# Attention into a feed-forward layer on one core: a new fixed order for the first two batches

## The chip, the cores and the metric

The kernel runs on one core of one Trainium2 chip. The metric is the device time of one execution in microseconds. Engines are named as in the profile: PE is TensorE (matmuls), PEld its weight loads, DVE VectorE, ACT ScalarE, POOL GpSimd, SP the sync engine, which here does nothing but issue DMAs. SPq and POOLq stand for the queue of an engine that issues DMAs.

## The reference, cut to what matters

```python
# B = 8 batches, H = 8 heads, 512 local and 32 global positions, head size D = 64
s_g   = q_g @ [k_g; k_l].T / 8                         # global rows see everything
out_g = softmax(s_g) @ [v_g; v_l]
s_ll  = q_l @ k_l.T / 8, masked to |i - j| <= 32       # local rows see a band ...
s_lg  = q_l @ k_g.T / 8                                # ... and the global keys
out_l = softmax([s_lg, s_ll]) @ [v_g; v_l]
x = concat(out_g, out_l), heads side by side           # 8 * 544 rows of 512
h = x @ w_in                                           # 512 -> 2048
out = (h * clip(h + 3, 0, 6) / 6) @ w_out              # 2048 -> 512
```

Inputs and the output are float32; the kernel works in float16 with float32 sums.

## The kernel before, in words

Work goes by pairs of heads: `p = 4 * batch + m`, 32 pairs, four per batch. For a pair:

- `load(p)` issues three DMAs of 256 KB (k, q, v, float32) on SP into staging tiles `stg`, of which there are 13 in turn. `cast(p, what, engine)` makes float16 of them (`kn`, `qn`, and the batch's `vt`) and frees the staging tile. `vshift(p)` copies half of v to other partitions (`vb`), `vglob(b)` puts the global v rows into `vb` and, except for batch 0, into `vgs`, `kglob(b)` the global keys into `kT`. `fill_v`, `ones_v` and `fill_vg` set up the constant parts of `vt`, `vb` and `vgs`, once for each of two buffers.
- `emit_T(p)` transposes k and q into `kT` and `qT`: batches 0 and 1 by TensorE through PSUM (lines 219 to 227), later ones by DMA transposes on SP (line 213), after which `qwrap` copies 32 columns of `qT` on GpSimd.
- `emit_S(p, ch)`, ch 0 and 1, makes band scores (`psS`, line 248) and their exponentials `E` on ScalarE. The band mask is added by two more matmuls ahead (`pe_mask`, line 242) or multiplied in afterwards by VectorE (line 254).
- `emit_SG(p)` makes the scores of the global rows, `emit_AV(p)` the local output `xn`, `emit_PG(p)` the global rows' product, summed over the batch in `pg`.
- `emit_X(p)` transposes `xn` into `xt`: batches 0 and 1 by TensorE, later ones by a DMA transpose on SP (line 322). `emit_XG(b)` ends the global rows of a batch.

The feed-forward layer of a batch is cut into 32 units by `moe_units`: 16 `u1(c)` (four matmuls from the four `xt` into `psH`, line 354; ScalarE line 359, VectorE line 361 give `gt`) and 16 `u2(t, c4)` (four matmuls into `po`, line 370; the fourth unit of an output tile t copies it, line 374, and issues its stores on SP, line 376). `units` is a list that is used from the front: `M(n)` emits the next n units between pieces of attention. The global rows of all batches go through the layer at the end. `load_w`/`cast_w` bring in and convert the weights in 16 pieces each; `load_g`/`emit_G` bring in, cast and transpose the global keys and queries of several batches, with 32 rows each.

Two things set the order. The code is traced in the order written, and `pin(engines)` ties everything traced since the last `pin` to that order on the engines named. Up to `pin(*ALL)` all five engines follow the code; afterwards only SP and GpSimd do (`pin(*QUEUES)`), and on TensorE, VectorE and ScalarE a planner takes what it holds to be ready, by its own estimates, earliest in the code first. Code after `pin(*ALL)` can also be planned ahead of pinned code.

The loop runs over p from 4 to 31. One iteration issues `load(p + 5)`, casts pair p + 4, does `emit_T(p + 3)`, and then, with the counts `n`: `M(n[0])`, `emit_S(p + 1, 0)`, `M(n[1])`, `emit_S(p + 1, 1)`, `emit_SG(p + 1)`, `M(n[2])`, `emit_AV(p)`, `emit_PG(p)`, `M(n[3])`, `emit_X(p)`. At the end of a batch its 32 units are appended.

Of the kernel before, what the change touches and what calls it, by code (L numbers as in the profile page):

```python
# [14 lines left out]
def kernel(  # L15
# [12 lines left out]
    nc = tc.nc  # L28
    P = 128
# [44 lines left out]
    NV = 2  # L74
# [74 lines left out]
    def load_vg(b):  # L149
        nc.gpsimd.dma_start(out=vg[rg, b], in_=v_g[b].rearrange("h s d -> s h d"))  # L150
# [22 lines left out]
    def load_g(b0, b1, nm):  # L173
        src = {"kg": k_g, "qg": q_g}[nm]
        t = stage()
        for b in range(b0, b1):
            i = b - b0
            nc.sync.dma_start(out=t[i * Sg:(i + 1) * Sg].rearrange("s (h d) -> s h d", h=H),
                              in_=src[b].rearrange("h s d -> s h d"))
        gst[b0, nm] = t  # L180
# [224 lines left out]
        load_w("in", i)  # L405
    for i in range(NC):
        load_w("out", i)
        if i == 3:
            load_g(1, 4, "kg")
            load_g(0, 4, "qg")  # L410
    for p in range(NM, 2 * NM + 1):
        load(p)

    make_identity(nc, ident)
    load_vg(0)
    mb = const("mb", [P, 2, P])
    ones = const("ones", [P, 1])
    nc.vector.memset(ones, 1.0)
    nc.vector.memset(mb, 0.0)
    nc.vector.memset(mb[D + Sg:P, 1], -30000.0)  # L420
# [21 lines left out]
    def fill_vg(i, eng):  # L442
        eng.memset(vgs[i], 0.0)
        eng.memset(vgs[i][rg, :, D:P], 1.0)

    fill_v(0, nc.vector)
    ones_v(0)
    nc.scalar.memzero(qgz)
# [2 lines left out]
    nc.vector.tensor_copy(out=mv, in_=mb.unsqueeze(2).to_broadcast([P, 2, NT, P]))  # L451
    nc.vector.memset(mv[:, 0, 0, 0:W], fill)
    nc.vector.memset(mv[0:D, 1, 0, W:P], fill)

    def first(p, what="kqv"):
        cast(p, what, nc.gpsimd)
        vshift(p, nc.gpsimd)

    first(0, "qv")
    load_vg(1)  # L460
    emit_T(0)
    emit_G(0, 1, "kg")
    kglob(0, nc.vector)
    vglob(0, nc.vector)
    units += moe_units(lambda mm: xts[0][mm], Sl, local_dests(0), early=True)
    u1 = units.pop(0)
    for p in range(1, NM):
        first(p)
    for i in range(NC):
        cast_w("in", i, nc.gpsimd)  # L470
    emit_S(0, 0, True)
    emit_T(1, True)
    emit_S(0, 1, True)
# [20 lines left out]
    emit_X(3)  # L494
    for c in range(HEAD):
        u1(c, range(3, 4))
    fill_vg(0, nc.vector)
    nc.vector.tensor_copy(out=vgs[0][rg, :, 0:D], in_=vg[rg, 0])
    for t in Egs:
        nc.vector.memset(t[:, NT], 0.0)  # L500
    nc.vector.tensor_scalar(out=mk.rearrange("p c w q -> p c (w q)"), in0=mneg, scalar1=-1.0,
                            scalar2=1.0, op0=is_ge, op1=mult)
    for c in range(HEAD, NC):
        u1(c)
    for i in range(NC):
        cast_w("out", i, nc.gpsimd)
    emit_G(1, 4, "kg")
    emit_G(0, 4, "qg")
    fill_v(1, nc.vector)
    fill_vg(1, nc.gpsimd)  # L510
    kglob(1, nc.gpsimd)
    vglob(1, nc.gpsimd)
    for p in range(NM, 2 * NM):
        cast(p, "k", nc.vector)
        cast(p, "qv", nc.gpsimd)
        vshift(p, nc.gpsimd)
    M(3)
    pin(*ALL)
    emit_T(4)
    emit_SG(0)  # L520
    emit_SG(1)
    M(1)
    emit_SG(2)
    emit_SG(3)
    emit_S(4, 0)
    M(1)
    for p in range(NM):
        emit_PG(p)
    emit_T(5)
    emit_S(4, 1)  # L530
    ones_v(1)
    emit_SG(4)
    emit_XG(0)
    for b in range(2, B):
        load_vg(b)

    for p in range(NM, NPAIR):
        b, m = divmod(p, NM)
        if p + 5 < NPAIR:
            load(p + 5)  # L540
        if p + 4 < NPAIR:
# [3 lines left out]
            vshift(p + 4, nc.gpsimd)  # L545
        if m == 1 and b + 1 < B:
            kglob(b + 1, nc.gpsimd)
        if p == 5:
            load_g(4, B, "kg")
            load_g(4, B, "qg")  # L550
        if p == 10:
            emit_G(4, B, "kg")
            emit_G(4, B, "qg")
        n = (1, m < 2, 0, 0) if b == 1 else (1, 2, 2, 3)
        if p + 3 >= 2 * NM:
            if 2 * NM <= p + 2 < NPAIR:
                qwrap(p + 2)
            if p + 3 < NPAIR:
                emit_T(p + 3)
        if p + 2 < 2 * NM:  # L560
            emit_T(p + 2)
        M(n[0])
        if p + 1 < NPAIR:
            emit_S(p + 1, 0)
# [49 lines left out]
```

## Time and profile before

| | |
|---|---|
| median of the runs | 341.62 us (341.24 to 342.2) |
| the profiled execution: span, first to last instruction | 341.3 us |
| TensorE busy | 313.4 us (92%), 2756 matmuls |
| VectorE, ScalarE, GpSimd busy | 214.9, 199.3, 133.3 us |
| TensorE busy, 0 to 90 us | 66.67 us |
| TensorE busy, 90 to 341.3 us | 246.74 us |
| traffic | 53.69 MB, on average 157 GB/s |

The profile is of one execution. Its page shows busy time by engine, the span in 40 slices, the chain of work that ended last, and the costliest groups; the trace behind it answers for any window which engine was busy, how long TensorE's granted clock was reduced (1.00 is full), and what an instruction waited for. A row of a group gives busy time and the mean of one in ns; a row of a timeline gives start, duration and, in brackets, the idle time before it with what ended it. In a row of windows each engine's busy time is followed by its number of instructions, and the last three numbers are clock, DMA share and GB/s.

### The profile page before, as it was taken

The numbers are of one execution on the slowest core, as the hardware profiler recorded it, in microseconds if no ns is written. First come the engines' busy times: TensorE is split into PE (matmuls) and PEld (weight loads), VectorE is DVE, ScalarE is ACT, GpSimd is POOL, SyncE is SP. The second block draws the span as 40 slices with busy tenths as digits, with TensorE's granted clock in tenths as the row PEclk, the third lists the DMA queues.
The fourth block names the chain that finished last, engine by engine and source line by source line (L and its number), as shares of the span: only waits on it lengthen the run. The fifth ranks groups of instructions, "written<-read, shape, count | busy, mean of one in ns | idle before, by whom it ended". The sixth has DMA issues, their size and how long they took to land.

```text
span 341.3 us, 7410 instructions
## 1 busy us (share of the span) xinstructions
PE 313.4 (92%) x2756; PEld 160.1 (47%) x2756; DVE 214.9 (63%) x488; ACT 199.3 (58%) x393; POOL 133.3 (39%) x240
## 2 busy tenths in 40 slices
PE   1999678855999999999999999999999999999994
PEld 0554235433454455545445454444544445444571
DVE  4678847755587469745884589448854784274170
ACT  8557419443586468645874587448844881382270
POOL 5985799936733453336323633264300000000000
PEclk9999989955999999999999999999999999999998
DMA  8998899979977989799779988999734112201102
GB/s 215 318 385 221 293 288 222 196 165 172 225 143 129 211 179 151 138 188 218 136 140 190 208 144 140 142 206 194 140 100 106 28 17 77 79 0 32 62 31 62
DMA packets 143011, 53.69 MB, mean 157 GB/s; under 512 B 130433, under 2 KB 134529, under 8 KB 142977
## 3 DMA queue, kind: packets, MB, share of 16 engines
q1 hardware_dynamic: 140800, 52.97, 71.8%
q0 software_dynamic: 2176, 0.26, 1.2%
q8 instruction: 21, 0.34, 0.5%
q14 instruction: 14, 0.11, 0.1%
HBM read 35.13 MB, written 8.91 MB: 129 GB/s over the span
## 4 chain that ended last, share of the span: by engine, by line
PE 83%; POOL 6%; ACT 3%; DVE 3%; DMA 3%; issue 1%; SPq 1%; POOLq 0%; DVEq 0%
PE psH L354 35%; PE po L370 33%; PE psS L248 5%; PE pav L288 2%; PE pav L291 2%; DMA stg<-in_v_l_dram 2%; PE psSG L265 2%; PE pg L311 1%; ACT vt L439 1%; POOL vb L145 1%; PE psS L242 1%; POOL qn L136 1%; POOL vg L150 1%; POOL vb L141 1%; POOL vt L136 1%
## 5 line engine op out<-in xcount | busy, mean ns | idle before, releaser
L370 PE MATMUL po<-wout,gt 128*128 128x512 f16 x544 | 128.3, 386 | 0.0
L354 PE MATMUL psH<-xt,win 128*128 128x512 f16 x512 | 117.3, 379 | 0.5 <-DVE xt L331 0.5
L361 DVE SCALAR_TENSOR_TENSOR gt<-t,psH 128x512 f16<-128x512 f32 (+1 forms) x144 | 90.8, 655 | 31.3 <-ACT t L359 30.5
L359 ACT ACTIVATE t<-psH,half_col 128x512 f32<-128x512 f32 (+1 forms) x144 | 92.2, 665 | 24.5 <-PE psH L354 21.9
L252 ACT ACTIVATE E<-psS 128x512 f16<-128x512 f32 x128 | 68.9, 596 | 62.8 <-PE psS L248 62.8
L354 PEld LDWEIGHTS <-win 128*128 128x128 f16 x576 | 53.5, 98 | 54.0 <-issue 0.6
L370 PEld LDWEIGHTS <-gt 128*128 128x128 f16 x544 | 50.9, 99 | 57.5 <-issue 4.0
L254 DVE TENSOR_TENSOR E<-E,mk 128x512 f16<-128x512 f16 x112 | 52.0, 483 | 23.8 <-ACT E L252 22.7
L136 POOL CAST kn<-stg 128x512 f16<-128x512 f32 x27 | 17.0, 630 | 53.6 <-DMA stg<-in_k_l_dram 50.3
L248 PE MATMUL psS<-qT,kT 64*128 64x128 f16 x512 | 27.0, 229 | 7.1 <-DVE qT L227 4.7
L374 DVE COPY ot<-po 128x512 f32<-128x512 f32 x17 | 11.8, 691 | 34.0 <-PE po L370 34.0
L248 PEld LDWEIGHTS <-kT 64*128 64x128 f16 x512 | 15.6, 98 | 33.5 <-issue 24.0
L374 ACT COPY ot<-po 128x512 f32<-128x512 f32 x17 | 10.0, 586 | 36.6 <-PE po L370 36.6
L297 DVE TENSOR_TENSOR xn<-pav,rc 128x256 f16<-128x256 f32 x64 | 26.0, 421 | 1.2
L145 POOL COPY vb<-vg 32x512 f16<-32x512 f16 x28 | 16.2, 616 | 22.5 <-issue 11.8
L136 POOL CAST qn<-stg 128x512 f16<-128x512 f32 x32 | 20.7, 646 | 10.3 <-DMA stg<-in_q_l_dram 10.0
L136 POOL CAST vt<-stg 128x512 f16<-128x512 f32 x32 | 19.9, 620 | 10.6 <-DMA stg<-in_v_l_dram 10.6
L141 POOL COPY vb<-vt 64x512 f16<-64x512 f16 x32 | 19.9, 623 | 2.1
L291 PE MATMUL pav<-vb,E 128*128 128x65 f16 x256 | 20.6, 197 | 0.0
L288 PE MATMUL pav<-vt,E 128*128 128x65 f16 x256 | 20.6, 196 | 0.0
L288 PEld LDWEIGHTS <-E 128*128 128x128 f16 x256 | 18.4, 100 | 3.1
L291 PEld LDWEIGHTS <-E 128*128 128x128 f16 x256 | 17.5, 99 | 2.8
(73 smaller groups left out, 213.4 us busy)
## 6 DMA issues: line engine op xcount, KB each, us to landing
stg<-in_k_l_dram SPq DMA_DIRECT2D x32, 256.0 KB, 3.7
stg<-in_q_l_dram SPq DMA_DIRECT2D x32, 256.0 KB, 4.3
stg<-in_v_l_dram SPq DMA_DIRECT2D x32, 256.0 KB, 4.9
out_dram<-ot SPq DMA_DIRECT2D x24, 256.0 KB, 2.3
stg<-in_moe_w_in_dram SPq DMA_DIRECT2D x16, 256.0 KB, 6.1
stg<-in_moe_w_out_dram SPq DMA_DIRECT2D x16, 256.0 KB, 4.9
out_dram<-ot SPq DMA_DIRECT2D x8, 192.0 KB, 2.6
out_dram<-ot SPq DMA_DIRECT2D x16, 64.0 KB, 1.9
```

The costliest lines, as they stand in the source:

```text
L136: eng.tensor_copy(out=o, in_=s[c + "f"])
L141: eng.tensor_copy(out=vbs[b % NV][0:D, :, hs, 0:D], in_=vts[b % NV][D:P, :, hs, 0:D])
L248: nc.tensor.matmul(out=pss[e][:, w * P:(w + 1) * P], lhsT=kT[r, c0:c0 + P], rhs=qT[r, w * P:(w + 1) * P], start=not pe_mask, stop=True, sk ...
L252: nc.scalar.activation(out=E[:, ch, e], in_=pss[e], func=EXP, scale=qk_scale)
L254: nc.vector.tensor_tensor(out=E[:, ch, e], in0=E[:, ch, e], in1=mk[:, ch].rearrange("p w c -> p (w c)"), op=mult)
L288: nc.tensor.matmul(out=o, lhsT=E[:, 0, e, w * P:(w + 1) * P], rhs=vt[:, w, h, 0:D + 1], start=True, stop=False, skip_group_check=True)
L291: nc.tensor.matmul(out=o, lhsT=E[:, 1, e, w * P:(w + 1) * P], rhs=vb[:, (w - 1) % NT, h, 0:D + 1], start=False, stop=True, skip_group_chec ...
L297: nc.vector.tensor_tensor(out=xn[:, 2 * w2:2 * w2 + 2].rearrange("p w (e d) -> p w e d", e=2), in0=pv[:, :, :, 0:D], in1=rc.to_broadcast([ ...
L354: nc.tensor.matmul(out=ps[:, 0:n], lhsT=w_in_t[m][:, c * P:(c + 1) * P], rhs=rhs(m), start=(m == 0), stop=(m == NM - 1), skip_group_check= ...
L359: nc.scalar.activation(out=t1[:, 0:n], in_=ps[:, 0:n], func=RELU, bias=half_col, scale=1.0 / 6.0)
L361: nc.vector.scalar_tensor_tensor(out=gts[c][:, 0:n], in0=t1[:, 0:n], scalar=1.0, in1=ps[:, 0:n], op0=amin, op1=mult)
L370: nc.tensor.matmul(out=po[t][:, 0:dm], lhsT=gts[c][:, t * P:(t + 1) * P], rhs=w_out_t[c // 4][:, c % 4], start=(c == 0), stop=(c == NC - 1))
```

## The change

The diff rewrites the part up to and including pair 7, and the counts of units after it.

- Loads: the k_g and q_g loads of batches 1 to 3 move from the middle of w_out to behind it, among pair 4's loads; those of batches 4 to 7 from p = 5 to p = 8. `load(9)` to `load(12)` are written between the pieces of the new order, ahead of the stores that follow. The v_g loads of batches 2 to 7, until now in a row, are spread.
- Idle matmuls: `warm(7)` before the first transposes and `warm(4)` after them multiply a tile of zeros into a PSUM tile that nobody reads.
- Fills: `fill_vg(0)` and `fill_vg(1)` go to GpSimd between the two halves of w_in's casts, `fill_v(1)` to VectorE between the first-layer units, `vglob` of batches 0 and 1 to ScalarE (`vglob_act`), `kglob(1)` to VectorE, all of batch 1's casts to GpSimd, `ones_v(1)` behind batch 0's first layer.
- Order: batch 0's 16 second-layer units are called by name, `UU((t, c4), ...)`, the first eight alternating between output tiles 0 and 1 by chunks of w_out; batch 1's attention is written between them; batch 1's first units (`v1`) follow. All of this is tied on all engines. `emit_S` of pairs 4, 5 and 7 uses mask matmuls.
- Loop: it starts at p = 7 with a special iteration, and the counts of batch 2 are (1, 1, 1, 3).

```diff
@@ -405,16 +405,20 @@
         load_w("in", i)
     for i in range(NC):
         load_w("out", i)
-        if i == 3:
-            load_g(1, 4, "kg")
-            load_g(0, 4, "qg")
-    for p in range(NM, 2 * NM + 1):
+    load_g(1, 4, "kg")
+    load(NM, "kq")
+    load_g(0, 4, "qg")
+    load(NM, "v")
+    for p in range(NM + 1, 2 * NM + 1):
         load(p)
 
     make_identity(nc, ident)
     load_vg(0)
+    load_vg(1)
+    wz = const("wz", [P, Sl])
     mb = const("mb", [P, 2, P])
     ones = const("ones", [P, 1])
+    nc.vector.memset(wz, 0.0)
     nc.vector.memset(ones, 1.0)
     nc.vector.memset(mb, 0.0)
     nc.vector.memset(mb[D + Sg:P, 1], -30000.0)
@@ -443,6 +447,16 @@
         eng.memset(vgs[i], 0.0)
         eng.memset(vgs[i][rg, :, D:P], 1.0)
 
+    def warm(n):
+        ps = ps_tile("psW")
+        for _ in range(n):
+            nc.tensor.matmul(out=ps, lhsT=wz[:, 0:P], rhs=wz, skip_group_check=True)
+
+    def vglob_act(b):
+        for u in range(NT):
+            nc.scalar.copy(out=vbs[b % NV][rg, u, :, 0:D], in_=vg[rg, b])
+
+    warm(7)
     fill_v(0, nc.vector)
     ones_v(0)
     nc.scalar.memzero(qgz)
@@ -451,23 +465,26 @@
     nc.vector.tensor_copy(out=mv, in_=mb.unsqueeze(2).to_broadcast([P, 2, NT, P]))
     nc.vector.memset(mv[:, 0, 0, 0:W], fill)
     nc.vector.memset(mv[0:D, 1, 0, W:P], fill)
-
-    def first(p, what="kqv"):
-        cast(p, what, nc.gpsimd)
-        vshift(p, nc.gpsimd)
-
-    first(0, "qv")
-    load_vg(1)
+    cast(0, "qv", nc.gpsimd)
+    vshift(0, nc.gpsimd)
     emit_T(0)
+    warm(4)
     emit_G(0, 1, "kg")
     kglob(0, nc.vector)
-    vglob(0, nc.vector)
+    vglob_act(0)
     units += moe_units(lambda mm: xts[0][mm], Sl, local_dests(0), early=True)
     u1 = units.pop(0)
     for p in range(1, NM):
-        first(p)
+        cast(p, "kqv", nc.gpsimd)
+        vshift(p, nc.gpsimd)
+    for i in range(NC // 2):
+        cast_w("in", i, nc.gpsimd)
+    fill_vg(0, nc.gpsimd)
+    fill_vg(1, nc.gpsimd)
+    for i in range(NC // 2, NC):
+        cast_w("in", i, nc.gpsimd)
     for i in range(NC):
-        cast_w("in", i, nc.gpsimd)
+        cast_w("out", i, nc.gpsimd)
     emit_S(0, 0, True)
     emit_T(1, True)
     emit_S(0, 1, True)
@@ -494,48 +511,121 @@
     emit_X(3)
     for c in range(HEAD):
         u1(c, range(3, 4))
-    fill_vg(0, nc.vector)
-    nc.vector.tensor_copy(out=vgs[0][rg, :, 0:D], in_=vg[rg, 0])
+    fill_v(1, nc.vector)
     for t in Egs:
         nc.vector.memset(t[:, NT], 0.0)
     nc.vector.tensor_scalar(out=mk.rearrange("p c w q -> p c (w q)"), in0=mneg, scalar1=-1.0,
                             scalar2=1.0, op0=is_ge, op1=mult)
     for c in range(HEAD, NC):
         u1(c)
-    for i in range(NC):
-        cast_w("out", i, nc.gpsimd)
+    for b in range(2):
+        nc.vector.tensor_copy(out=vgs[b][rg, :, 0:D], in_=vg[rg, b])
+    vglob_act(1)
+    ones_v(1)
+    U = {(t, c4): units[t * (NC // 4) + c4] for t in range(NT) for c4 in range(NC // 4)}
+    units.clear()
+
+    def UU(*tc):
+        for t, c4 in tc:
+            U[t, c4]()
+
+    UU((0, 0), (1, 0), (0, 1), (1, 1), (0, 2), (1, 2))
     emit_G(1, 4, "kg")
+    kglob(1, nc.vector)
+    for p in range(NM, 2 * NM):
+        cast(p, "kqv", nc.gpsimd)
+        vshift(p, nc.gpsimd)
+    load(9)
+    UU((0, 3), (1, 3))
+    emit_T(4)
+    UU((2, 0))
+    emit_S(4, 0, True)
+    emit_S(4, 1, True)
     emit_G(0, 4, "qg")
-    fill_v(1, nc.vector)
-    fill_vg(1, nc.gpsimd)
-    kglob(1, nc.gpsimd)
-    vglob(1, nc.gpsimd)
+    emit_SG(0)
+    UU((2, 1))
+    emit_T(5)
+    emit_SG(1)
+    load(10)
+    UU((2, 2))
+    emit_AV(4)
+    emit_S(5, 0, True)
+    emit_S(5, 1, True)
+    emit_SG(2)
+    emit_PG(0)
+    UU((2, 3))
+    emit_X(4)
+    load(11)
+    for b in (2, 3):
+        load_vg(b)
+    emit_T(6)
+    emit_AV(5)
+    emit_SG(3)
+    UU((3, 0))
+    emit_S(6, 0)
+    emit_S(6, 1)
+    emit_PG(1)
+    emit_X(5)
+    UU((3, 1))
+    cast(8, "kqv", nc.gpsimd)
+    cast(9, "kq", nc.gpsimd)
+    emit_T(7)
+    emit_PG(2)
+    UU((3, 2))
+    emit_AV(6)
+    emit_S(7, 0, True)
+    emit_S(7, 1, True)
+    emit_PG(3)
+    emit_XG(0)
+    kglob(2, nc.gpsimd)
+    vshift(8, nc.gpsimd)
+    vglob(2, nc.gpsimd)
+    emit_T(8)
+    qwrap(8)
+    load(12)
+    cast(9, "v", nc.gpsimd)
+    vshift(9, nc.gpsimd)
+    UU((3, 3))
+    emit_X(6)
+    emit_SG(4)
+    emit_SG(5)
+    units += moe_units(lambda mm: xts[1][mm], Sl, local_dests(1), early=True)
+    v1 = units.pop(0)
+    for c in range(HEAD):
+        v1(c, range(2))
+    emit_AV(7)
+    emit_SG(6)
+    emit_SG(7)
+    for c in range(HEAD):
+        v1(c, range(2, 3))
+    emit_X(7)
+    for c in range(HEAD):
+        v1(c, range(3, 4))
     for p in range(NM, 2 * NM):
-        cast(p, "k", nc.vector)
-        cast(p, "qv", nc.gpsimd)
-        vshift(p, nc.gpsimd)
-    M(3)
+        emit_PG(p)
+    emit_XG(1)
+    units[:0] = [lambda c=c: v1(c) for c in range(HEAD, NC)]
     pin(*ALL)
-    emit_T(4)
-    emit_SG(0)
-    emit_SG(1)
-    M(1)
-    emit_SG(2)
-    emit_SG(3)
-    emit_S(4, 0)
-    M(1)
-    for p in range(NM):
-        emit_PG(p)
-    emit_T(5)
-    emit_S(4, 1)
-    ones_v(1)
-    emit_SG(4)
-    emit_XG(0)
-    for b in range(2, B):
-        load_vg(b)
-
-    for p in range(NM, NPAIR):
-        b, m = divmod(p, NM)
+
+    for p in range(2 * NM - 1, NPAIR):
+        b, m = divmod(p, NM)
+        first = p < 2 * NM
+        if p == 7:
+            emit_T(9)
+            for q in (10, 11):
+                cast(q, "kqv", nc.gpsimd)
+                vshift(q, nc.gpsimd)
+                if q == 10:
+                    qwrap(9)
+                    emit_T(10)
+            M(3)
+            emit_S(8, 0)
+            M(1)
+            emit_S(8, 1)
+            emit_SG(8)
+            M(1)
+            pin(*QUEUES)
+            continue
         if p + 5 < NPAIR:
             load(p + 5)
         if p + 4 < NPAIR:
@@ -545,20 +635,19 @@
             vshift(p + 4, nc.gpsimd)
         if m == 1 and b + 1 < B:
             kglob(b + 1, nc.gpsimd)
-        if p == 5:
+        if p == 8:
             load_g(4, B, "kg")
             load_g(4, B, "qg")
+        if m == 2 and b + 2 < B:
+            load_vg(b + 2)
         if p == 10:
             emit_G(4, B, "kg")
             emit_G(4, B, "qg")
-        n = (1, m < 2, 0, 0) if b == 1 else (1, 2, 2, 3)
-        if p + 3 >= 2 * NM:
-            if 2 * NM <= p + 2 < NPAIR:
-                qwrap(p + 2)
-            if p + 3 < NPAIR:
-                emit_T(p + 3)
-        if p + 2 < 2 * NM:
-            emit_T(p + 2)
+        n = (1, 1, 1, 3) if b == 2 else (1, 2, 2, 3)
+        if p + 2 < NPAIR:
+            qwrap(p + 2)
+        if p + 3 < NPAIR:
+            emit_T(p + 3)
         M(n[0])
         if p + 1 < NPAIR:
             emit_S(p + 1, 0)
```

## The prediction

> **What bounds the kernel now.** I read the windows first, cut where the slices of the page show holes, then the chain of waits inside them, then the timelines of the queues that the chain names.
>
> ```profile
> span 341.3 us, 7410 instructions
> ```
> ```profile
> 38.00:92.30 54.30, 39.04 (x449) 22.37 (x450) 33.19 (x80) 24.99 (x60) 42.52 (x71) 0.81 1.09 213
> 42.00:46.00 4.00, 4.00 (x13) 1.51 (x11) 2.60 (x6) 0.00 (x0) 3.06 (x5) 0.57 0.93 252
> 70.00:86.00 16.00, 10.25 (x116) 6.64 (x117) 9.77 (x25) 7.05 (x17) 7.62 (x14) 0.50 1.14 174
> 92.30:336.80 244.50, 244.44 (x2048) 122.50 (x2046) 154.63 (x337) 148.25 (x291) 63.52 (x119) 1.00 0.63 126
> 336.80:341.30 4.50, 0.00 (x0) 0.00 (x0) 0.00 (x0) 0.56 (x1) 0.00 (x0) 0.75 0.23 58
> ```
>
> The second column is the busy time of TensorE, the third from the right its granted clock. From 92.3 to 336.8 us TensorE is busy in 244.44 of 244.50 us at full clock: there the end is set by the amount of matmul work, and that work stays. From 38.0 to 92.3 it is busy in 39.04 of 54.30 us, and part of that at 0.50 and 0.57 of the clock. This stretch (last w_out casts, batch 1's attention, second half of batch 0's feed-forward) is what the new order rewrites. The chain says what held it:
>
> ```profile
> 37.97 0.70 ACT t L359
> 39.30 0.70 DVE kgn L185
> 41.79 3.83 PE po L370 x10
> 45.68 2.24 POOL vb L145 x4
> 68.03 2.32 DMA stg<-in_k_g_dram
> 75.05 6.26 DMA stg<-in_v_l_dram
> 89.67 3.45 PE psH L354 x16
> 93.12 0.33 PE psS L248 x8
> 124.75 3.46 PE psH L354 x16
> 133.41 3.46 PE psH L354 x16
> ```
>
> At 38 the order demands the transposes of k_g (line 185) straight after the last first-layer unit, while VectorE still drains; from 45 to 66 GpSimd is the path (vglob, then batch 1's casts); at 68 VectorE sits in front of a k_g load that was only just issued, and pair 7's q wrap is queued behind it; at 75 a v load. From 89.67 on, one pair with eight units takes 8.66 us (133.41 less 124.75); a unit of four matmuls takes 0.864 (3.45 over four), so a pair's attention takes 1.75.
>
> **The change part by part. A, the start.**
>
> ```profile
> 5.14 2.04 ACT vt L439 x4
> 8.71 0.96 PE psS L242 x2
> 20.62 0.43 PE psS L242 x2
> 25.90 12.05 PE psH L354 x55
> ```
> ```profile
> 4.96 0.61 PE L219 MATMUL psTq<-ident,qn 128*128 128x128 f16 x4 [0.33 <-POOL qn L136]
> 14.34 0.61 POOL L136 CAST qn<-stg 128x512 f16<-128x512 f32 x1
> 22.11 5.32 POOL L169 CAST win<-stg 128x512 f16<-128x512 f32 x8 [0.98 <-DMA stg<-in_moe_w_in_dram]
> 42.76 0.62 POOL L169 CAST wout<-stg 128x512 f16<-128x512 f32 x1 [0.95 <-DMA stg<-in_moe_w_out_dram]
> 43.31 0.95 POOL L443 MEMSET vgs<- 128x1024 f16 x1
> 44.32 0.52 POOL L444 MEMSET vgs<- 32x512 f16 x1
> ```
>
> ScalarE now does the four copies of ones_v(1) at 5.14 although they are not due until batch 1; psTq is ready at 5.57, so qT loses 1.6 us. The new code pins these copies behind the first layer. VectorE is rid of vglob; ScalarE gets it, four copies at the 0.51 of an L439 copy, 2.0 us, between qT (6.2) and the first exponential (8.4), hidden behind the G and S matmuls. It waits for the v_g load, and behind it on ScalarE stand all exponentials: without the cover it costs its 2.0. The 7 and 4 idle matmuls take 0.48 each at the half speed of the first psS pair (0.96 for two, 0.43 later): 3.4 us before the first transposes and 1.9 after psTq, both inside TensorE idle time, at worst 0.5 of delay to psTk. The second v_g load, moved ahead of the mask builds, costs 0.6 of GpSimd there and gives it back before pair 1's casts. So S(0,0) comes 1.2 to 1.9 earlier, but pair 3's q cast, now ending at 14.95, moves only by that 0.6. From that cast to the start of the long first-layer run there are 11 us now; I allow 9. Gain 2.5 us; ends 0 (GpSimd's casts pace it all) and 4.
>
> As to the clock, the Trainium skill ("TensorE: Matmul & The Clock Gate", Part 1) says that about 3.4 us of sustained activity lifts the engine from half to full speed; the trace agrees in the sizes 0.96 and 0.43, and no run here shows idle matmuls. By that rule S(0,0) would run at full speed, an estimate of 1 us more gain at most, which the paced casts take back.
>
> The two fill_vg, moved between w_in 7 and w_in 8, put 2 × 1.47 us on GpSimd; 0.98 of it falls into its wait there. w_in 15 is cast at about 29 (27.4 now), while the first layer wants it at about 32: hidden, and worth 2 us if that slack were gone.
>
> **B, the stretch from 38.**
>
> ```profile
> 26.83 3.01 SPq L178 DMA_DIRECT2D stg<-in_q_g_dram  x4
> 30.53 9.82 SPq L160 DMA_DIRECT2D stg<-in_moe_w_out_dram  x12
> 41.36 0.38 SPq L120 DMA_DIRECT2D stg<-in_k_l_dram  x1
> ```
> ```profile
> stg<-in_k_l_dram SPq DMA_DIRECT2D x32, 256.0 KB, 3.7
> ```
> ```profile
> 14.00:26.00 12.00, 11.21 (x157) 6.42 (x157) 7.54 (x24) 6.58 (x13) 10.39 (x18) 1.00 1.05 384
> 28.00:32.00 4.00, 4.00 (x21) 1.82 (x19) 3.70 (x12) 2.70 (x5) 1.94 (x4) 1.00 0.72 105
> ```
>
> Seven small k_g and q_g loads sit between w_out 3 and 4 (the row at 26.83 is four of them): the traffic falls from 384 to 105 GB/s, the last w_out is cast at 43.4. Moved behind w_out, the weights stream on: 0.262 MB at 384 GB/s is 0.68 us, sixteen from 27.4 (end of the w_in casts) land by 38.3. GpSimd, at 0.61 a cast from 29, ends at 38.8, 4.6 earlier. The first six second-layer units, taken over two output tiles, want chunks 0 to 11 alone and fill 5.2 us meanwhile, at the price of a second open bank. SP then issues k_g at about 33, pair 4's k and q at 35 (41.36 now; landing 3.7 later, when GpSimd comes free), then q_g (3.0 us of issue: the 105 GB/s dip is now here, some 3 us of waiting for v) and the rest. GpSimd, rid of kglob and vglob (to VectorE and ScalarE, both with idle time), needs 4 × 0.61 a pair from 39: 3 + 2.45 + two casts give pair 5's q at 46, three pairs more than pair 4 pair 7's v at 52. The new TensorE order wants pair 5 at 47, pair 6 at 52, pair 7 at 56, v of pair 7 at 62: the loads are ahead, narrowly for pair 5. load(9) to load(11) are issued before the stores they used to follow, and load_g(4) moves to p = 8, so the block at 68 goes. Next on GpSimd, vglob(2) waits for PG(3), at about 61, with pair 8's q wrap and pair 9's v cast behind it; S(8,0), which wants the wrap, comes at about 68.
>
> The work is priced by what was done. 39.04 us busy, less the slow parts: 4.00 at 0.57 is 2.3, 10.25 at 0.50 is 5.1, so 32.2 us at full clock. Masks on TensorE for S(4), S(5), S(7) add six pairs at 0.43, 2.6 us (and take masks from VectorE, which is not the bound). What stays late: the kgn cast (0.70) right before its transposes, SG(0) right after G(0,4) with two qgz copies between, and first products behind T copies, each put at 0.9 by that cast: 2.5 us. Together 37.3 instead of 54.3: gain 17.0. Ends: 19.5 without these waits, 9 if batch 1 comes as late against the weights as now.
>
> **C, batch 2's pairs.** With no half-idle stretch before them, pairs 8 to 11 carry six units each and last 6 × 0.864 + 1.75 = 6.9 us instead of 8.66. SP must issue for each:
>
> ```profile
> 110.77 0.57 SPq L123 DMA_DIRECT2D stg<-in_k_l_dram  x1
> 112.80 1.51 SPq L213 DMA_TRANSPOSE kT<-kn  x1
> 114.42 1.20 SPq L213 DMA_TRANSPOSE qT<-qn  x1
> 115.71 1.47 SPq L376 DMA_DIRECT2D out_dram<-ot  x3
> 117.63 1.22 SPq L322 DMA_TRANSPOSE xt<-xn  x1
> 66.12 2.37 SPq L178 DMA_DIRECT2D stg<-in_k_g_dram  x4
> ```
>
> Three loads 1.7, two transposes 2.7, xt 1.2, about one store 0.5: 6.1 us; over four pairs 24.4, and 2 × 2.37 for the moved k_g and q_g loads, 29.1 against 27.6. I charge 2 us; ends 0 (transposes run two pairs ahead) and 7 (the pace of 8.66 stays, 4 × 1.76).
>
> **D, the seams between batches.** Now five units of a batch are still open when the next batch's last xt is transposed (11 of 16 are called by p = 7, then eight a pair), and they cover it: the last xt of batch 2 is issued at 117.63 and its first use is at 124.75. The new counts come out even: 29 units after p = 6, 5 at p = 7, 24 over p = 8 to 11, nothing over. So the last unit's store now stands on SP directly ahead of the last xt of each batch, and the next batch's first unit needs that xt. From the last unit's end: ot copy, store, transpose.
>
> ```profile
> L374 ACT COPY ot<-po 128x512 f32<-128x512 f32 x17 | 10.0, 586 | 36.6 <-PE po L370 36.6
> DMA to landing us min/median/max: 2.4/2.8/4.3
> ```
>
> 0.59 + 0.5 + 2.8 with 0.5 of gaps: 4.4 us, six times (batches 2 to 7). Against it stand matmuls that don't need that xt: three of four of each open unit (0.65 us, up to five units in the seven banks, 3.2) and S and SG of the next pair (0.8). The planner is free to order these. The row nearest is 93.12: the code has S(9,0) ahead of the first units of batch 1, the trace has sixteen of their matmuls before it, so the planner does run other work where it expects a DMA to be late. I take 1.0 us a seam, 6 in all; ends 0 and 4.4 each.
>
> The end (4.5 us after the last matmul) is the same. **Sum:** 341.3 − 2.5 − 17.0 + 2 + 6 = 329.8 for the profiled execution. The median of the runs, 341.62, stands 0.3 above its span, but the ends of A and B lean a little to more gain, since TensorE's 39.04 holds the drained tails of each stop; I say 329.5.
>
> **The rivals.**
> 1. *The seams are filled.* For it: the reordering at 93.12. D is 0 and C about 1: 322.5.
> 2. *Batch 2 keeps its pace of 8.66* because SP or the DMA engines don't give more: DMA share 1.09 from 38 to 92. Against it: share 0.63 afterwards, and loads five pairs ahead. C is 7: 335.
> 3. *The seams run in code order: slower.* Each costs 4.4 less the first unit's 0.65, 3.75 us, and then the clock: after the idle time at 38 to 41.4 ten po matmuls took 3.83 instead of 2.16, 1.7 more. Six times 5.4 is 32.7 in place of 6: 356; without the clock 346. It decides from 2.9 us a seam (19.5 gained less C's 2 is 17.5, over six). Against it: 93.12 again. The Trainium skill (the same page, the table of its last part) asks for no idle gap above about 3 us, since the clock halves after one; the trace agrees with its 0.57 after 38, and by that rule 3.75 would be over the line.
> 4. *Batch 1 is bound by its loads as now*, the stops only change place: B is 9: 337.5. Against it: k of pair 4 can be issued 6 us sooner.
>
> **How the numbers follow.** The forecast (325 to 334) has 0.40, rival 1 (317 to 325) 0.25, rival 2 0.12, rival 4 0.10, rival 3 0.10, no change that can be told, within 0.3%, 0.03. The spread of the runs before makes 0.3% about what can be told. Leaving out half of the lowest case's tail and rival 3, the range is 318 to 341; the likeliest case's own is 325 to 334. Faster: 0.87; same 0.03; slower 0.10.
>
> **What would show it.** A: the long psH run starts near 23.4 and ends near 35.5. B: clock 1.0 from 15 us on without a half-clock window, last wout cast near 39, batch 1's first psH near 64 (89.67 now), no stop over 2 us. C: S(9) to S(12) 6.9 us apart. D: gaps of TensorE before the fourth psH of each batch, about 1 us, none over 3. If the seams show 3 us and more with a clock under 1, or if TensorE stands between 66 and 95 behind kT and qT transposes, the forecast is wrong.

## The result, and the profile after

The changed kernel takes 332.98 us (median of four runs, 332.18 to 334.47) where the kernel before took 341.91 beside it: a ratio of 0.9737, 95% interval 0.9706 to 0.9769. 329.5 was forecast, with a range of 318 to 341. The profiled execution took 332.45 us and has a span of 330.6. In the profiled executions of the changed kernel and of all experiments the time is 1.8 to 2.1 us above the span (1.7 to 2.5 over all executions), so the span of 341.3 before belongs, by that estimate, to a time of about 343. That is some 1.4 above that kernel's median, as 341.3 is above its median span of about 340 in the 62 executions timed beside the experiments. The spans shown differ by 10.7 us, the medians by 8.9.

The windows of the kernel after, cut where its stages end (columns as before: TensorE's busy time second, then weight loads, VectorE, ScalarE, GpSimd, granted clock, DMA share, GB/s):

```profile
0.00:36.50 36.50, 32.05 (x272) 15.73 (x273) 25.50 (x70) 25.99 (x43) 31.05 (x59) 1.00 1.04 324
36.50:66.80 30.30, 29.17 (x350) 16.65 (x349) 16.53 (x45) 21.81 (x50) 20.38 (x34) 1.00 1.12 243
66.80:97.07 30.27, 26.28 (x297) 14.14 (x295) 24.29 (x49) 21.03 (x44) 19.21 (x34) 1.00 0.99 169
97.07:126.64 29.57, 27.66 (x248) 13.64 (x245) 19.39 (x45) 18.79 (x39) 13.79 (x25) 1.00 1.09 189
126.64:325.00 198.36, 197.09 (x1625) 98.58 (x1623) 116.25 (x264) 114.09 (x227) 48.11 (x90) 1.00 0.60 119
325.00:330.60 5.60, 0.00 (x0) 0.00 (x0) 0.00 (x0) 0.58 (x1) 0.00 (x0) 0.72 0.20 50
```

The half-clock windows are gone, and the idle time behind 36.5 us is 1.1, 4.0, 1.9 and 1.3 us in the four stages, 8.3 in all; the kernel before has 15.3 from 38 to 92.3 and almost none later. The last matmul ends at 325.0 (336.8 before); the tail behind it is 1.1 longer. The chain of work, its longest pieces:

```profile
24.46 12.03 PE psH L354 x55
36.49 5.18 PE po L370 x24
66.83 4.04 DMA qT<-qn
73.35 2.88 DMA qT<-qn
82.39 2.72 DMA stg<-in_k_g_dram
111.23 3.66 DMA xt<-xn
126.64 0.86 PE po L370 x4
145.06 2.43 DMA xt<-xn
161.62 0.86 PE po L370 x4
180.46 2.60 DMA xt<-xn
318.06 6.92 PE po L370 x32
```

No load and no GpSimd cast stands in it between 36 and 66 us, where vglob and the casts stood before. Transposes of pairs 8 and 9 do from 66 to 76, and at each seam between batches (111, 145, 180) a transpose of xt. From 126.64 to 161.62 a batch takes 34.98 us.

### The profile page after: what moved, and what is told of

Read it like the earlier page. It is cut to its first block, busy times and chain, and to the rows that moved or that the text cites. A ratio compares the mean times of both kernels' runs of the same rounds, so it can differ in the third digit from the quotient of the medians.

```text
span 330.6 us, 7444 instructions
## 1 busy us (share of the span) xinstructions
PE 312.2 (94%) x2779; PEld 158.7 (48%) x2779; DVE 202.0 (61%) x469; ACT 202.3 (61%) x401; POOL 132.5 (40%) x240
## 4 chain that ended last, share of the span: by engine, by line
PE 79%; DMA 8%; DVE 4%; ACT 3%; SPq 3%; POOL 2%; issue 1%; POOLq 0%; DVEq 0%; ACTq 0%
PE po L370 36%; PE psH L354 28%; PE psS L248 5%; DMA xt<-xn 4%; DMA qT<-qn 2%; PE pav L288 2%; PE pav L291 2%; PE psSG L265 2%; DMA stg<-in_v_l_dram 1%; PE pg L311 1%; ACT E L252 1%; PE psS L242 1%; SPq L123 1%; DVE gt L361 1%; DMA stg<-in_k_g_dram 1%
## 5 line engine op out<-in xcount | busy, mean ns | idle before, releaser
L370 PE MATMUL po<-wout,gt 128*128 128x512 f16 x544 | 126.3, 379 | 0.0
L354 PE MATMUL psH<-xt,win 128*128 128x512 f16 x512 | 119.6, 379 | 4.0 <-DMA xt<-xn 2.9
L361 DVE SCALAR_TENSOR_TENSOR gt<-t,psH 128x512 f16<-128x512 f32 (+1 forms) x144 | 87.9, 652 | 24.9 <-ACT t L359 24.1
L359 ACT ACTIVATE t<-psH,half_col 128x512 f32<-128x512 f32 (+1 forms) x144 | 89.0, 668 | 21.5 <-PE psH L354 19.2
L254 DVE TENSOR_TENSOR E<-E,mk 128x512 f16<-128x512 f16 x100 | 46.9, 484 | 51.3 <-ACT E L252 49.3
L370 PEld LDWEIGHTS <-gt 128*128 128x128 f16 x544 | 49.8, 97 | 54.4
L136 POOL CAST kn<-stg 128x512 f16<-128x512 f32 x31 | 19.6, 633 | 53.5 <-DMA stg<-in_k_l_dram 52.8
L248 PE MATMUL psS<-qT,kT 64*128 64x128 f16 x512 | 25.4, 218 | 2.7 <-DMA stg<-in_k_g_dram 1.8
L136 POOL CAST vt<-stg 128x512 f16<-128x512 f32 x32 | 19.9, 621 | 11.8 <-DMA stg<-in_v_l_dram 11.7
L145 POOL COPY vb<-vg 32x512 f16<-32x512 f16 x24 | 14.2, 630 | 13.5 <-PE pav L291 7.7
L288 PEld LDWEIGHTS <-E 128*128 128x128 f16 x256 | 17.8, 97 | 3.7 <-ACT ot L374 0.3
L291 PEld LDWEIGHTS <-E 128*128 128x128 f16 x256 | 16.8, 97 | 3.3 <-issue 0.2
```

Source lines behind the costliest of these rows:

```text
L136: eng.tensor_copy(out=o, in_=s[c + "f"])
L248: nc.tensor.matmul(out=pss[e][:, w * P:(w + 1) * P], lhsT=kT[r, c0:c0 + P], rhs=qT[r, w * P:(w + 1) * P], start=not pe_mask, stop=True, sk ...
L254: nc.vector.tensor_tensor(out=E[:, ch, e], in0=E[:, ch, e], in1=mk[:, ch].rearrange("p w c -> p (w c)"), op=mult)
L288: nc.tensor.matmul(out=o, lhsT=E[:, 0, e, w * P:(w + 1) * P], rhs=vt[:, w, h, 0:D + 1], start=True, stop=False, skip_group_check=True)
L291: nc.tensor.matmul(out=o, lhsT=E[:, 1, e, w * P:(w + 1) * P], rhs=vb[:, (w - 1) % NT, h, 0:D + 1], start=False, stop=True, skip_group_chec ...
L354: nc.tensor.matmul(out=ps[:, 0:n], lhsT=w_in_t[m][:, c * P:(c + 1) * P], rhs=rhs(m), start=(m == 0), stop=(m == NM - 1), skip_group_check= ...
```

## The experiments

Three theories were set against each other. Theory 1: the new written order, tied on all engines, with the w_out chunks and late g loads, carries the gain. Theory 2: GpSimd's queue, freed of fills and v_g copies and reached earlier by the loads, carries it. Theory 3: units held back as cover between the pieces of batch 1's attention carry it. Ratios are to the kernel before, timed beside each; the kernel after is 0.9737. An interval is 0.5 to 1.4 us wide to either side, so two changed kernels that differ by less than about 1.5 us can't be told apart by their times; smaller differences are given below, but rest on the traces.

**Idle matmuls out.** After, with the calls `warm(7)` and `warm(4)` removed.

```diff
-    warm(7)
...
-    warm(4)
```

> The changed kernel without both calls of idle matmuls. If the gain came from taking waits out of the stretch from 38 us on (theory 1), the idle matmuls matter little: the first matmuls run at half speed until about 14 us, the long first-layer run starts near 25.5 instead of 24.5, and the time is 1 us longer, about 334. If the clock at the start is a main part of the gain (rival), the run starts at 26 or later and the time is over 335.5. Under 333.3 the idle matmuls do nothing.

Measured: 332.86 us, 0.9746 (0.9705 to 0.9787), the same as the kernel after. TensorE's timeline, first of the kernel after, then of this one (start, duration, idle time before in brackets):

```profile
1.20 3.17 PE L453 MATMUL psW<-wz 128*128 128x512 f16 x7 [1.20 <-DVE ones L422]
7.18 0.60 PE L242 MATMUL psS<-mneg,ident 128*128 128x512 f16 x2
```
```profile
7.04 1.03 PE L242 MATMUL psS<-mneg,ident 128*128 128x512 f16 x2
10.53 1.06 PE L242 MATMUL psS<-mneg,ident 128*128 128x512 f16 x2
13.04 0.59 PE L242 MATMUL psS<-mneg,ident 128*128 128x512 f16 x2
```

The idle matmuls do what the prediction took from the Trainium skill ("TensorE: Matmul & The Clock Gate", Part 1): behind the two groups of them (3.17 and 1.56 us) the first mask pair takes 0.60 instead of 1.03 us. They bring nothing: the medians agree. The long first-layer run starts at 25.19 without them and at 24.46 in the profile with them, but in both it starts 10.38 us after GpSimd begins pair 3's q cast (14.81 and 14.08). That start is paced by GpSimd's casts, as the forecast said.

**Open units over the seams.** After, with batch 2's counts lowered by one, so that four units are left over at each end of a batch.

```diff
-        n = (1, 1, 1, 3) if b == 2 else (1, 2, 2, 3)
+        n = (1, 1, 1, 2) if b == 2 else (1, 2, 2, 3)
```

> The changed kernel with counts (1, 1, 1, 2) for batch 2, so that four units of a batch stay open when the next batch's last xt is transposed. If the stops at the seams are real losses (theory 1), the 1.8 us before batch 2's fourth group of psH and the some 0.3 us at the five later seams go, in all about 3 us: 330. If the planner had filled them already and the time is only moved (rival), it stays within 1 us of 333.

Measured: 331.82 us, 0.9704 (0.9673 to 0.9736), span 328.1; about 1.1 us below the kernel after, less than the intervals' width, but the chain shows the mechanism:

```profile
110.83 3.45 DMA xt<-xn
128.19 0.86 PE po L370 x4
162.84 0.86 PE po L370 x4
```

The transposes at 145 and 180 have left the chain, and a batch takes 34.65 us (162.84 less 128.19) instead of 34.98. The first seam, at 111, stays.

**Pair 8's transposes early.** After, with pair 8's k and q casts and `emit_T(8)` moved up to ahead of `load(10)`.

```diff
+    cast(8, "kq", nc.gpsimd)
+    emit_T(8)
     load(10)
...
-    cast(8, "kqv", nc.gpsimd)
+    cast(8, "v", nc.gpsimd)
...
-    emit_T(8)
```

> The changed kernel with pair 8's k and q cast and their DMA transposes issued ahead of load(10), instead of behind load(10), load(11) and a store. If pairs 8 to 10 are late because GpSimd stands 7.4 us in front of pair 8's q wrap (theory 1), that wait falls under 2 us, S(10) moves from 85 to about 80, TensorE's idle time between 66.8 and 97 falls from 4.0 to about 1.5 us, and the time is about 330.5. If batch 2's pairs are bound by the DMA engines (rival), loads 10 and 11 come as much later as the transposes come earlier, and the time stays within 1 us of 333.

Measured: 333.78 us, 0.9756 (0.9722 to 0.9791): no gain. Pair 8's q wrap ran at 64.74 instead of 71.02, and the wait stood one pair later; the row of GpSimd:

```profile
78.18 0.21 POOL L231 COPY qT<-qT 128x32 f16<-128x32 f16 x1 [8.54 <-DMA qT<-qn]
```

**The g loads back amid w_out.** After, with the loads of k_g (batches 1 to 3) and q_g (batches 0 to 3) where they were before.

```diff
     for i in range(NC):
         load_w("out", i)
-    load_g(1, 4, "kg")
+        if i == 3:
+            load_g(1, 4, "kg")
+            load_g(0, 4, "qg")
     load(NM, "kq")
-    load_g(0, 4, "qg")
```

> The changed kernel with the k_g and q_g loads of batches 0 to 3 back in the middle of w_out. If the order of the loads carries part B (theory 1), the last w_out cast moves from 38.5 back to 42 to 43, TensorE waits some 3 us for it ahead of the fourth chunk, pair 4's casts start 2 to 4 us later, and the time is 336 to 337. If the loads are hidden and only the order of the engines counts (rival), it stays within 1 us of 333.

Measured: 335.39 us, 0.9798 (0.9759 to 0.9836), 2.4 us lost by the medians, between the two expectations. Not all of it comes from the loads. Three of the six executions take 333.5 to 334.5 us at a mean granted clock of 0.993 to 0.999, where the kernel after has 0.992 to 0.999; the other three take 336.3 to 337.6 us at 0.984 to 0.987. The profiled execution is the slowest of these, and its half-clock window, which the last section shows, is over at about 18 us, before SP issues the first of the moved loads at 25.44. The first three alone have a median 0.8 above the kernel after. From 36.5 to 66.8 TensorE is busy in 27.57 of 30.30 us (29.17 in the kernel after), with a stop of 1.48 us for pair 4's q cast.

**The order left free.** After, with `pin(*QUEUES)` in place of `pin(*ALL)` behind the new order: the planner may reorder TensorE, VectorE and ScalarE.

```diff
-    pin(*ALL)
+    pin(*QUEUES)
```

> The changed kernel with the first two batches tied on SP and GpSimd alone; TensorE, VectorE and ScalarE are left to the planner there. If the order written out for all engines is what takes the waits out of 36 to 67 us (theory 1), stops of several us and a half-clock window come back there and the time is 337 or more. If the loads, the casts and the fills bring the gain and the planner finds an order as good (rival), it stays within 1.5 us of 333.

Measured: 334.14 us, 0.9777 (0.975 to 0.9803): 1.2 us are lost by the medians, as the rival had it. Theory 1 falls so far as the tying is meant: the planner, given the new text, finds nearly the same time.

**Parts alone, in the kernel before.** First the g loads moved behind w_out, then those of batches 4 to 7 from p = 5 to p = 8, then ScalarE's `ones_v(1)` written behind the first layer.

```diff
-        if i == 3:
-            load_g(1, 4, "kg")
-            load_g(0, 4, "qg")
+    load_g(1, 4, "kg")
+    load_g(0, 4, "qg")
```

> The kernel before with one part of the change: the k_g and q_g loads of batches 0 to 3 behind w_out. If the loads' order is a gain by itself (theory 1), the last w_out cast moves from 43.4 to about 39, GpSimd's chain of casts from 45 to 66 moves up by 4, and the time is about 338. If the old order of TensorE can't use it (rival), k_g now arrives after 38 us where its transposes stand straight behind the first layer, TensorE waits there 1 to 2 us longer, and the time is 341 to 344.

```diff
-        if p == 5:
+        if p == 8:
             load_g(4, B, "kg")
```

> The kernel before with one part of the change: the k_g and q_g loads of batches 4 to 7 at p = 8 instead of p = 5. Theory 1: the block at 66 to 71 us (4.4 us of TensorE) goes, pairs 7 and 8 come 4 us earlier, and with less of the half-clock window 336 to 338. Rival: the v load that stands next in the chain (75 to 81) is late for another reason, the wait moves there, and the time is 340 to 342.

```diff
         vshift(p, nc.gpsimd)
+    ones_v(1)
     M(3)
...
-    ones_v(1)
```

> The kernel before with one part of the change: ones_v(1) tied behind batch 0's first layer, so that its four copies no longer stand ahead of the first qT. Theory 1: qT and the first scores come 1.5 us earlier, but pair 3's casts on GpSimd pace the rest, so that the long first-layer run starts 0.5 to 1 us earlier: 341. Rival (the copies were on the path in full): 2 us earlier, 340.

Measured: 340.44 (0.9969, 0.9949 to 0.9989), 342.2 (1.0017, 0.9989 to 1.0044; one execution of 1737.97 us is left out of the ratio) and 341.22 (1.0000, 0.9981 to 1.0019). Moved alone, one of these gives 1 us and two give nothing. In the first, both expectations came true in part: the last w_out cast starts at 39.41 instead of 42.76, and TensorE's stop ahead of the k_g transposes (`kgn` is the float16 copy that they read, `qgn` that of q_g) grows from 2.11 to 3.74 us:

```profile
41.25 0.46 PE L188 MATMUL psGT<-ident,kgn 96*128 96x96 f16 x4 [3.74 <-DVE kgn L185]
```

The second did remove the stop behind the k_g load, and the chain shows what came instead:

```profile
72.63 4.56 DMA qT<-qn
84.25 2.60 PE psH L354 x12
```

Batch 1's first psH in the chain starts 5.4 us earlier than the 89.67 of before, and the span of 339.5 is still an ordinary one of the kernel before. In the third the long run starts at 26.01, as before (25.90): the four copies on ScalarE cost nothing there.

**GpSimd's queue undone.** After, with `fill_vg(1)`, `kglob(1)` and `vglob(1)` on GpSimd again, ahead of batch 1's casts.

```diff
-    fill_vg(1, nc.gpsimd)
...
-    vglob_act(1)
...
-    kglob(1, nc.vector)
+    fill_vg(1, nc.gpsimd)
+    kglob(1, nc.gpsimd)
+    vglob(1, nc.gpsimd)
```

> The changed kernel with one part undone: fill_vg(1), kglob(1) and vglob(1) are back on GpSimd in front of batch 1's casts (5 us of work). e5 showed that tying the other engines is not what brings the gain. If GpSimd's queue ahead of batch 1's casts is (theory 2), pair 4's casts move from 41 to 45 or 46, pairs 5 to 7 follow, TensorE stops for 3 to 4 us before T(4), and the time is 336 to 337. If TensorE's other work in between covers it (rival), it stays within 1 us of 333.

**And the same done to the kernel before,** together with the g loads behind w_out.

```diff
+        if i == 7:
+            fill_vg(1, nc.gpsimd)
...
-    fill_vg(1, nc.gpsimd)
-    kglob(1, nc.gpsimd)
-    vglob(1, nc.gpsimd)
+    nc.vector.tensor_copy(out=vgs[1][rg, :, 0:D], in_=vg[rg, 1])
+    kglob(1, nc.vector)
+    for u in range(NT):
+        nc.scalar.copy(out=vbs[1][rg, u, :, 0:D], in_=vg[rg, 1])
```

> The kernel before with two parts of the change together: the k_g and q_g loads behind w_out (e6: 1 us), and fill_vg(1), kglob(1), vglob(1) out of GpSimd's way as in the change. Theory 2 (what batch 1's casts wait for carries the gain, in whatever order): pair 4's q cast comes at 41 instead of 48.5, batch 1's attention ends 5 us earlier, and the time is 336 to 337. Rival (the old written order, with the second-layer units used up early and nothing left to run beside batch 1 and pair 8, keeps the loss): 339 to 341.

Measured: 333.72 us, 0.9761 (0.9745 to 0.9777) and 340.08, 0.9945 (0.9926 to 0.9963). Undone, the queue costs 0.7 us, within what the intervals can tell; done in the kernel before, with the loads, it gives 1.9. Both are what the rivals had, and theory 2 falls. In the first, pair 4's k cast is 6.2 us later than in the kernel after (40.78), and TensorE loses 3 us there and finds them again behind it. GpSimd's row, and the windows of TensorE:

```profile
47.00 0.61 POOL L136 CAST kn<-stg 128x512 f16<-128x512 f32 x1
```
```profile
36.50:66.80 30.30, 26.16 (x269) 13.77 (x267) 15.53 (x34) 14.88 (x32) 24.19 (x40) 0.94 1.13 242
66.80:97.00 30.20, 28.27 (x326) 15.44 (x325) 23.98 (x56) 24.00 (x53) 18.61 (x33) 1.00 0.96 161
97.00:126.00 29.00, 28.74 (x274) 14.46 (x275) 18.60 (x44) 18.32 (x39) 13.39 (x25) 1.00 1.20 195
```

In the second, the loads that come later meet the old order, which asks for the transposes of k_g straight behind the first layer. TensorE's timeline, and its windows:

```profile
40.53 0.50 PE L188 MATMUL psGT<-ident,kgn 96*128 96x96 f16 x4 [3.31 <-DVE kgn L185]
42.22 5.56 PE L370 MATMUL po<-wout,gt 128*128 128x512 f16 x14
```
```profile
36.50:66.80 30.30, 24.78 (x285) 13.44 (x283) 21.66 (x51) 17.22 (x40) 22.31 (x35) 0.89 1.12 222
66.80:97.00 30.20, 24.06 (x243) 13.05 (x244) 19.40 (x47) 17.55 (x37) 16.72 (x31) 0.77 0.98 187
```

The stop of 3.31 us is followed by fourteen po matmuls in 5.56 us, 0.40 each, where the kernel after does them in 0.216 (5.18 over 24). In the new order six units stand ahead of that transpose. In the old order the loads and the freed queue are worth little (0.3% and, together, 0.6%); the new order keeps 2.0% of its 2.6% without the one and 2.4% without the other.

**Open units and late loads.** The second experiment, with `load(11)` and `load(12)` moved behind the transposes of pairs 8 and 10 on SP.

```diff
-    load(11)
...
-    load(12)
+    load(11)
...
                     emit_T(10)
+            load(12)
```

> e2 (four open units over the seams) with load(11) behind pair 8's transposes and load(12) behind those of pairs 9 and 10. e3 moved only pair 8's and the wait came back at pair 9's q wrap. If the order on SP makes pairs 8 to 10 late (theory 1), q wrap 8 comes at 66 instead of 71, that of pair 9 at about 70, S(10) at 81 or before, TensorE's idle time from 66.8 to 97 falls under 1.5 us and the time is 1.5 to 2.5 us under e2's 331.8. If these pairs are bound by the DMA engines (rival), it equals e2 within 1 us.

Measured: 331.53 us, 0.9704 (0.967 to 0.9738), equal to the second experiment's. The wraps came earlier (66.72 and 73.53; 71.02 and 76.38 in the kernel after) and the time did not.

**The held-back units up front.** After, with the eight units of output tiles 2 and 3 called together.

```diff
     UU((0, 3), (1, 3))
+    for i in range(NC // 4):
+        UU((2, i), (3, i))
...
-    UU((2, 0))
...
-    UU((3, 3))
```

> The kernel after, with one edit: the eight units of batch 0's second layer for output tiles 2 and 3 are called together, right behind those for tiles 0 and 1, instead of one by one between the pieces of batch 1's attention. Loads, casts, copies and their order on the other queues stay. Theory 3 (the gain of the stretch from 38 us comes from holding units back as cover): batch 1's attention then runs without cover. The eight units are 8 x 0.864 = 6.9 us of matmuls that stood in TensorE's waits; some of the pieces move forward into the room that they leave, so I expect half to most of it lost: 3 to 6 us, 336 to 339, with TensorE waits of over 1 us at T(5) to T(7), at kgn or qgn and at the exponentials between 45 and 65 us, and batch 1's first psH still at 62 to 65. If the stops grow past 3 us the granted clock falls to 0.50 in the stretch and it is 340 or more. Rival (the place of the units does not matter, since the attention pieces wait for casts and loads whichever way they are called, and later batches have slack): within 1.5 us of the kernel after, 332 to 334.5.

Measured: 334.6 us, 0.9786 (0.9759 to 0.9813); 1.6 us above the kernel after, between the two expectations and just past the rival's 334.5. The windows:

```profile
36.50:66.80 30.30, 26.51 (x292) 14.87 (x291) 15.67 (x39) 17.61 (x38) 20.94 (x34) 1.00 1.04 244
66.80:97.00 30.20, 27.86 (x322) 15.39 (x321) 23.82 (x52) 22.94 (x52) 19.02 (x33) 1.00 0.87 168
```

Without cover TensorE loses 2.7 us in batch 1's attention (26.51 busy, 29.17 in the kernel after), in stops of at most 0.95 us, and gets 1.6 back in the next window. Batch 1's first psH comes at 67.47, later than expected. Theory 3 holds in kind, for a small part of the gain.

**What holds pairs 8 to 10.** Several experiments brought something earlier or later, and most of it was given back between 66 and 111 us. The traces show a place that they have in common. The rows of GpSimd and of TensorE in the kernel after, and last the row of S(10) in the run with open units over the seams:

```profile
71.02 0.21 POOL L231 COPY qT<-qT 128x32 f16<-128x32 f16 x1 [7.36 <-DMA qT<-qn]
76.38 0.21 POOL L231 COPY qT<-qT 128x32 f16<-128x32 f16 x1 [1.20 <-DMA qT<-qn]
79.05 2.76 POOL L145 COPY vb<-vg 32x512 f16<-32x512 f16 x4
84.89 0.21 POOL L231 COPY qT<-qT 128x32 f16<-128x32 f16 x1
```
```profile
71.28 0.40 PE L248 MATMUL psS<-qT,kT 64*128 64x128 f16 x8
76.64 0.40 PE L248 MATMUL psS<-qT,kT 64*128 64x128 f16 x8 [0.88 <-POOL qT L231]
85.15 0.40 PE L248 MATMUL psS<-qT,kT 64*128 64x128 f16 x8 [1.75 <-DMA stg<-in_k_g_dram]
92.74 0.40 PE L188 MATMUL psGT<-ident,qgn 128*128 128x128 f16 x4 [0.99 <-DVE qgn L185]
93.93 0.40 PE L248 MATMUL psS<-qT,kT 64*128 64x128 f16 x8
100.61 0.40 PE L248 MATMUL psS<-qT,kT 64*128 64x128 f16 x8
```
```profile
85.04 0.40 PE L248 MATMUL psS<-qT,kT 64*128 64x128 f16 x8 [1.75 <-POOL qT L231]
```

The scores of pairs 8, 9 and 10 each begin 0.26 us after the start of their wrap; TensorE stands idle ahead of the second (0.88 us) and the third (1.75). The third wait is put down to a k_g load, which these matmuls do not read and which landed in the same moment; the wrap at 84.89 is what they need. With open units over the seams the same wait of 1.75 us is put down to the wrap itself, at 84.78. In the kernel after the wrap shows no wait of its own: GpSimd comes straight from vglob(3) (the row at 79.05) and the casts of pair 12, which the code has ahead of it. In the experiment with pair 8 early and in the last one the third wrap starts at 86.68 and 87.04, and S(10) at 86.94 and 87.30, 0.26 later both times. With late loads it starts at 82.96 and S(10) at 83.22, and the gain of 1.9 is lost again at the first seam, where the transpose of xt is still in the chain (111.57, 3.07 us). So behind the wrap stands the next one, the DMA of that xt. That the wrap holds S(10) is read from these rows; moving it ahead of vglob(3) and the casts was not tried.

## Why the prediction was right, and where its terms were off

The sum for the span was 329.8 and the span is 330.6. The measured time is 3.5 above the 329.5 that was given: 0.8 for the sum, 0.6 for the lean to more gain that was taken off at the end, and 2.1 because a median was taken to stand 0.3 above the span, where it stands 2.4 above it (1.85 in the profiled execution itself, and that one is 0.5 below the median). That step, from span to median, was the weakest one; the 341.3 that it went by was 1.4 above an ordinary span.

- **A, the start: forecast 2.5, measured 1.4 in this profile** (24.46 for 25.90, as the end of the run, 36.49 for 37.95). Pair 3's q cast came 0.3 earlier instead of 0.6, and from its end to the run are 9.8 us instead of the 9 allowed. The 1.4 is one draw: in the profiles of the changed kernels with the order tied the run starts between 24.32 and 27.05. It also bought little. With open units over the seams the run starts at 25.80, 1.3 later, and the three wraps start at 71.03, 75.64 and 84.78, where the kernel after has 71.02, 76.38 and 84.89. ScalarE's copies, with which the part began, cost nothing: moved alone they changed nothing.
- **B, the stretch from 38: forecast 17.0, measured about 17.5.** This is what remains of the 11.8 us by which the last matmul ends earlier, after A's 1.4, C's loss of 4.0 and D's of 3.2. The signs held: the last w_out cast starts at 38.52 (39 forecast), batch 1's first psH at 63.33 (64), pair 5's q cast at 45.74 (46), pair 7's v at 51.83 (52), no stop over 2 us and no half clock from 15 us on. Waits of 2.5 were charged, 1.1 were found up to 66.8. But the argument behind it, link by link, is not how the gain hangs together: earlier casts are worth 0.7, the tied order 1.2, units as cover 1.6, the place of the g loads 0.8 to 2.4, and in the old kernel parts of the change give 0 to 1.9. Removed links are partly made good by the next, because TensorE has work in hand until the q wraps of pairs 8 to 10, and added links alone meet the next stop. By elimination the largest part belongs to what no run undid, the order of the text itself: six units ahead of the k_g transposes, batch 1's attention between the units, and its first layer begun early, on the xt of its first pairs. This is argued and not shown, since parts that make good for one another can't be summed. The stops of 3.74 and 3.31 in the old order with the new loads speak for the first. The exact place of batch 1's first psH weighs little: at 69.83 (queue undone) and 67.47 (units up front) instead of 63.33 the times are 0.7 and 1.6 longer, while in the old order it comes at 86.53 even with two parts of the change. How much each gives is open.
- **C, batch 2's pairs: forecast 2, measured 4.0** (26.28 busy of 30.27). 6.9 us were expected from S(9) to S(12) for each pair; the starts at 76.64, 85.15, 93.93 and 100.61 are 8.5, 8.8 and 6.7 apart. Two of three keep rival 2's pace, the third has the forecast one. The first holds the stop of 1.75 ahead of S(10). The second does not hang on a wrap (pair 11's starts at 88.82, S(11) at 93.93): it holds the transposes of the global keys and queries of batches 4 to 7 and a stop of 0.99 for VectorE's cast of the queries (the row at 92.74), which the sum left out. The step that failed was to ask only SP and the DMA engines. SP's queue was priced in full, but GpSimd's was followed to pair 9 and not to the third wrap behind vglob(3) and pair 12's casts. One of the prediction's own signs of being wrong also showed, in small: TensorE stands 0.88 ahead of S(9) for a wrap that itself waits for the transpose of q (the row at 76.38).
- **D, the seams: forecast 6, measured 3.2**, of it 1.9 in the first and 1.3 in the five others. The mechanism is the one described: the seams' transposes are in the chain at 111, 145 and 180, and with four units left over the later ones vanish from it. The planner's fill was under-rated: 0.3 a seam instead of 1.0, except where batch 2 begins. Rival 3, written order in the seams, did not happen. Its reading of the clock was loose, too: ahead of the 0.57 from 42 to 46 us in the kernel before stand idle times of 2.11 and 1.00 us with transposes of 0.34 between them, no single gap above 3.
- **The tail,** forecast unchanged, is 1.1 longer.

A, C and the tail came out 1.1, 2.0 and 1.1 worse than forecast, D 2.8 better, and B, which as the remainder closes the account, 0.5 better. That the sum is within 0.8 of the span is in that measure luck; B, by far the largest term, came out close.

## What to carry to other kernels

When a start-up stretch is rewritten, price it by the work that is left in it, as B was, and do not expect a single edit of the set to show its share: here parts of it in the old kernel gave 0 to 1.9 us and taken away from the new one cost 0 to 2.4, of 8.9. Follow every in-order queue to the point where the stretch ends, the small copies behind long casts too; here the scores of one pair waited 1.75 us for a copy of 0.21 us. Compare spans with spans: the distance from a span to its own execution's time was steady (1.7 to 2.5 us), the distance to a median was not.

## What the hardware showed beside this

Idle matmuls raise the clock early, but do not always keep it up. The windows of the kernel with open units over the seams, then of that with g loads amid w_out, then of the kernel after:

```profile
10.00:12.00 2.00, 1.00 (x14) 0.53 (x12) 0.97 (x3) 1.08 (x2) 1.87 (x4) 0.86 1.20 277
12.00:14.00 2.00, 2.00 (x17) 0.94 (x15) 0.88 (x2) 0.59 (x1) 1.68 (x4) 0.50 1.20 285
```
```profile
12.00:14.00 2.00, 2.00 (x14) 0.95 (x15) 0.88 (x2) 0.59 (x2) 1.69 (x4) 0.50 1.20 296
16.00:18.00 2.00, 2.00 (x25) 1.74 (x25) 1.39 (x5) 1.07 (x2) 1.94 (x4) 0.50 1.05 391
```
```profile
10.00:12.00 2.00, 0.88 (x13) 0.45 (x12) 0.83 (x3) 1.09 (x2) 1.84 (x4) 1.00 1.20 278
```

The three have the same idle matmuls and the same sparse work before 12 us, about half busy. In two the clock falls to 0.50 for a time and the long run starts at 25.80 and 27.05; in the third it stays at 1.00 and the run starts at 24.46. In the second experiment no idle time of TensorE before the fall is over 1.24 us. The Trainium skill ("TensorE: Matmul & The Clock Gate", the table of its last part) warns of idle gaps above about 3 us; here the clock fell without one, after some microseconds of half-busy work, and the trace decides. The record of the granted clock is also no guide in the first microseconds: it reads 1.00 in the kernel without idle matmuls while its first mask pairs take 1.03 and 1.06 us, and 0.59 later.
